# A 128-byte shift of the weight ring: padding behind the inverse-transform table of an attention and spectral-mixing kernel

## The chip, the cores and the metric

The kernel runs on one core of one Trainium2 chip. A core has a matrix engine (PE, or TensorE), a vector engine (DVE), a scalar engine (ACT), a general engine (POOL, or GpSimd) and a synchronising engine (SP); they run side by side and meet at semaphores. Sixteen DMA engines carry data between the chip's main memory and the core's working memory, which has 128 partitions. An address below is a byte offset within a partition; a tile of so many bytes per partition occupies the same offsets in all of them. Matrix products are summed in a second, small memory, PSUM.

The metric is the device time of one execution in microseconds (us), lower is better. A comparison counts as faster or slower from a difference of 2% on.

## The reference

Causal attention with a bias that decays with a running sum, followed by a spectral mixing layer: a Fourier transform over the sequence, one complex matrix per frequency for 64 frequencies, the inverse transform, a residual, and a channel product with a ReLU. Cut to what matters:

```python
def _attn_ref(q, k, v, s):                      # q, k, v: (8, 8, 576, 64)
    scores = scale * np.matmul(q, k.transpose(0, 1, 3, 2))
    cum = np.cumsum(np.maximum(s, 0.0), axis=-1)
    bias = -(cum[:, :, :, None] - cum[:, :, None, :])
    scores = np.where(causal, -1e9, scores + np.minimum(bias, 0.0))
    # ... softmax over the keys ...
    return np.matmul(attn, v)

def _moe_ref(x, w_r, w_i, w_ch):                # x: (8, 576, 512); w_r, w_i: (64, 512, 512)
    X = np.fft.rfft(x, axis=1)
    Xr, Xi = np.real(X[:, :64]), np.imag(X[:, :64])
    Yr = np.einsum('bmd,mde->bme', Xr, w_r) - np.einsum('bmd,mde->bme', Xi, w_i)
    Yi = np.einsum('bmd,mde->bme', Xr, w_i) + np.einsum('bmd,mde->bme', Xi, w_r)
    y = np.fft.irfft(Y, n=S, axis=1)            # Y is zero beyond 64 frequencies
    u = x + y
    return u + np.maximum(u @ w_ch, 0.0)
```

The two weight arrays hold 64 x 512 x 512 float32 numbers each, 67 MB, and each number is used once for each of the eight batches. They are by far the most of what has to be read.

## The kernel before

All tiles that live through the whole kernel come from one pool, in this order, and the weight ring comes right behind them:

```python
    gp = ctx.enter_context(tc.tile_pool(name="globals", bufs=1))
    x_all = gp.tile([P, NG, B, NT, P], FP16, name="x_all")
    y_acc = gp.tile([P, NCK, DM], FP32, name="y_acc")
    xs = [gp.tile([P, 2, 2, 2, 2, B, HM], BF16, name=f"xs{i}") for i in range(2)]
    # ...
    ident16h = gp.tile([P, P], FP16, name="ident16h")
    Ff_sb = gp.tile([P, NT, 3 * NM], FP16, name="Ff_sb")
    G_sb = gp.tile([P, S], FP16, name="G_sb")
    wch_sb = gp.tile([P, DT, DM], FP16, name="wch_sb")
    wpool = ctx.enter_context(tc.tile_pool(name="w_sb", bufs=WA))      # WA = 11
    wpool2 = ctx.enter_context(tc.tile_pool(name="w2_sb", bufs=WB))    # WB = 6
```

Here P = 128, S = 576, DM = 512, NT = 5 and SP = NT * P = 640. `G_sb` is the table of the inverse transform: 128 rows (64 frequencies, real and imaginary) of 576 half-precision numbers, which is 1152 bytes per partition. Places are given out one behind the other, so the length of `G_sb` sets where all later tiles begin.

A weight tile has 4096 bytes per partition. The weights are read as float32 and written as bfloat16 by transfers that POOL issues, two for each tile, each filling 64 partitions with two rows of 2048 bytes. The first eight tiles lie in parts of `y_acc` and `x_all` that aren't needed yet; all later ones lie in the ring:

```python
    def loads_w(upto):
            # ...
            i = ring_of(len(wt))
            if i is None:
                t = early[len(wt)]
            else:
                t = (wpool, wpool2)[i].tile([P, WM, DM], BF16, name="w_sb", tag="w")
            # ...
            for h in range(2):
                first = 1 if ri == 1 and m0 + h == 0 else 0
                todo.append((
                    t[HP * h : HP * h + HP, 2 * first :].rearrange("p (m q) e -> p m (q e)", q=2),
                    src[m0 + h + 2 * first : m0 + MC // 2 : 2, g * P : (g + 1) * P, :].rearrange(
                        "m (p q) e -> p m (q e)", q=2
                    ),
                ))
    # ...
        for _, (dst, src) in sorted(todo, key=lambda t: t[0]):
            nc.gpsimd.dma_start(out=dst, in_=src)            # L234: weights, q, k and v
```

The attention's own tiles come behind the ring: q, k and v, also loaded at L234, and the tile `v4` for the last 64 tokens of v:

```python
    v2 = [ap_.tile([P, 2 * NWN * W + P], FP16, name=f"v2_{i}") for i in range(NV)]
    v4 = [ap_.tile([P, B, VW], FP16, name=f"v4_{i}") for i in range(2)]      # VW = 66
    # ...
    t = loaded[n] = loaded[n + 1] = qkpool.tile([P, 2, R * D], BF16, name="qk2", tag="qk2")
```

The products with the weights (L463) start as soon as a tile has landed. After the last weight tile comes the end of the kernel: the inverse transform reads `G_sb` as stationary operand, and the results are summed in slots of the same ring and stored:

```python
    def add_y(dst, i, which, rows=slice(0, P), start=False, xx=(0, 1)):
            # ...
                nc.tensor.matmul(                                             # L744
                    dst[x][r, :], G_sb[rows, bass.ds(T * P, r.stop - r.start)],
                    yv[rows, bb, which, :], start=start, stop=True, skip_group_check=True,
                    tile_position=(0, r.start),
                )
    # ...
    def result(i):
        if i == 0:
            t = finpool.tile([P, 4 * DM], BF16, name="r_sb", tag="r", bufs=3)
        else:
            t = wpool.tile([P, WM, DM], BF16, name="r_w", tag="w").rearrange("p m e -> p (m e)")
        return t.bitcast(FP32).rearrange("p (x e) -> p x e", x=2)
    # ...
            dst = out[b, bass.ds(first_token(b, T + (x or 0)), P * (2 if x is None else 1)), :]
            nc.sync.dma_start(out=dst.rearrange("(x p) e -> p x e", p=P), in_=o)    # L828
```

Of the kernel before, what the change touches and what calls it, by code (L numbers as in the profile page):

```python
# [10 lines left out]
FP16 = mybir.dt.float16  # L11
# [7 lines left out]
def kernel(  # L19
# [11 lines left out]
    nc = tc.nc  # L31
    B, H, S, D = q.shape
    NM = moe_w_r.shape[0]
    DM = H * D
    P = 128
# [6 lines left out]
    SP = NT * P  # L42
# [45 lines left out]
    d_G = nc.inline_tensor(G_np, name="c_Ginv").ap()  # L88
# [8 lines left out]
    gp = ctx.enter_context(tc.tile_pool(name="globals", bufs=1))  # L97
# [6 lines left out]
    xs_flat = [t.rearrange("p q k h r b m -> p (q k h r b m)") for t in xs]  # L104
    ident16h = gp.tile([P, P], FP16, name="ident16h")
    Ff_sb = gp.tile([P, NT, 3 * NM], FP16, name="Ff_sb")
    G_sb = gp.tile([P, S], FP16, name="G_sb")
    wch_sb = gp.tile([P, DT, DM], FP16, name="wch_sb")
    wpool = ctx.enter_context(tc.tile_pool(name="w_sb", bufs=WA))
    wpool2 = ctx.enter_context(tc.tile_pool(name="w2_sb", bufs=WB))  # L110
# [154 lines left out]
    load(loads_w(W0), loads_v(0) + loads_tails(0) + first[2:] + loads_v(1))  # L265
    nc.sync.dma_start(out=Ff_sb, in_=d_Ff.rearrange("(T p) c -> p T c", p=P))
    nc.sync.dma_start(out=ident16h, in_=d_ident16h)
    nc.sync.dma_start(out=G_sb, in_=d_G)

    zero = ap_.tile([P, 16], FP32, name="zero")  # L270
    nc.vector.memset(zero, 0.0)
# [15 lines left out]
    with tc.tile_pool(name="cum_psum", bufs=1, space=PSUM) as cpsum:  # L287
# [5 lines left out]
            out=cum, data0=spos, data1=zer, initial=0.0, op0=ALU.add, op1=ALU.add  # L293
# [16 lines left out]
        for x in range(2):  # L310
            rows = slice(NL * x, NL * x + NL)
            nc.vector.tensor_copy(
                out=cumt4[rows, :], in_=cumt_sb[rows, NK, x::2]
# [653 lines left out]
```

## Time and profile before

| What | Value |
|---|---|
| time, median of 3 runs | 445.85 us (445.59 to 446.06) |
| span of the profiled execution | 443.9 us |
| PE busy | 339.8 us (77%) |
| DVE busy | 253.0 us (57%) |
| POOL busy | 246.2 us (55%) |
| ACT busy | 226.1 us (51%) |
| weight transfer of 256 KB from issue to landing, real and imaginary part | 8.4 and 8.9 us |
| store of 512 KB from issue to landing | 3.3 us |

The busy time of an engine is the time in which it works on an instruction; an engine that is idle in between waits for another one or for a transfer. The table alone doesn't tell which of them sets the time. For that, one has to see what the DMA engines do over the span, and which waits stand in the chain of work that ended last. GB/s in the profile count the bytes as written; where a transfer turns float32 into a 16-bit type, it reads twice as many. KB of a transfer are counted in the same way.

### The profile page before, as it was taken

The numbers are of one execution on the slowest core, as the hardware profiler recorded it, in microseconds if no ns is written. First come the engines' busy times: TensorE is split into PE (matmuls) and PEld (weight loads), VectorE is DVE, ScalarE is ACT, GpSimd is POOL, SyncE is SP. The second block draws the span as 40 slices with busy tenths as digits, with TensorE's granted clock in tenths as the row PEclk, the third lists the DMA queues.
The fourth block names the chain that finished last, engine by engine and source line by source line (L and its number), as shares of the span: only waits on it lengthen the run. The fifth ranks groups of instructions, "written<-read, shape, count | busy, mean of one in ns | idle before, by whom it ended". The sixth has DMA issues, their size and how long they took to land.

```text
span 443.9 us, 10783 instructions
## 1 busy us (share of the span) xinstructions
PE 339.8 (77%) x4364; PEld 206.9 (47%) x4411; DVE 253.0 (57%) x574; ACT 226.1 (51%) x421; POOL 246.2 (55%) x385
## 2 busy tenths in 40 slices
PE   1787888988686996593947828888887896859993
PEld 0465655656354553362625515565553455423441
DVE  7677775667545664462633605767655455432795
ACT  1477885467544743472633505765650444321793
POOL 7766666555565656365656546465544444530594
PEclk9999998999969898888895968999997999988998
DMA  9999999999999999999999999999999999996598
GB/s 181 202 207 205 204 207 205 206 206 205 209 192 205 205 209 204 209 206 208 204 207 206 209 206 202 206 206 203 205 209 210 210 209 210 209 217 122 179 373 324
DMA packets 72768, 93.25 MB, mean 210 GB/s; under 512 B 29760, under 2 KB 31296, under 8 KB 72720
## 3 DMA queue, kind: packets, MB, share of 16 engines
q0 software_dynamic: 63408, 81.29, 104.5%
q1 hardware_dynamic: 9312, 11.29, 7.8%
q8 instruction: 34, 0.56, 0.5%
q14 instruction: 14, 0.11, 0.1%
HBM read 163.51 MB, written 9.44 MB: 390 GB/s over the span
## 4 chain that ended last, share of the span: by engine, by line
DMA 67%; PE 16%; POOL 6%; DVE 5%; issue 4%; ACT 1%; POOLq 0%; DVEq 0%
DMA w_sb<-in_moe_w_i_dram 36%; DMA w_sb<-in_moe_w_r_dram 16%; DMA qk<-in_k_dram 10%; PE yp L463 3%; DMA x_all<-in_moe_w_r_dram 2%; POOL w_sb L234 2%; PE sc_ps L382 2%; DMA y_acc<-in_moe_w_r_dram 2%; PE sc_ps L376 2%; PE tr_ps L340 1%; POOL v L234 1%; PE u_ps L774 1%; PE av_ps L418 1%; PE z_ps L744 1%; DVE qt L344 1%
## 5 line engine op out<-in xcount | busy, mean ns | idle before, releaser
L390 ACT ACTIVATE p_sb<-sc_ps,cumt_sb 128x576 f16<-128x576 f32 (+1 forms) x256 | 141.5, 635 | 33.2 <-PE sc_ps L382 32.8
L234 POOL DMA_DIRECT2D w_sb<-in_moe_w_r_dram x120 | 71.2, 595 | 60.3 <-DMA w_sb<-in_moe_w_i_dram 16.1
L234 POOL DMA_DIRECT2D w_sb<-in_moe_w_i_dram x120 | 71.0, 593 | 53.2 <-DMA w_sb<-in_moe_w_i_dram 21.9
L344 DVE COPY qt<-tr_ps 64x576 bf16<-64x576 bf16 x64 | 47.8, 747 | 58.6 <-PE tr_ps L340 58.6
L234 POOL DMA_DIRECT2D v<-in_v_dram x72 | 52.0, 722 | 40.2 <-DMA w_sb<-in_moe_w_r_dram 9.6
L382 PE MATMUL sc_ps<-qt,kt 128*128 128x320 bf16 (+2 forms) x337 | 66.5, 302 | 6.7 <-ACT kt L344 2.7
L340 PE MATMUL tr_ps<-ident,qk 64*64 64x64 bf16 x1152 | 35.3, 206 | 40.9 <-DMA qk<-in_k_dram 17.6
L463 PE MATMUL yp<-w_sb,xs 128*32 128x512 bf16 (+1 forms) x480 | 43.2, 412 | 23.4 <-DMA w_sb<-in_moe_w_i_dram 16.6
L361 ACT ACTIVATE p<-sc_ps,cumt 128x64 f16<-128x64 f32 x32 | 10.0, 313 | 90.0 <-PE sc_ps L357 90.0
L376 PE MATMUL sc_ps<-negm,ident 128*128 128x256 bf16 x256 | 54.2, 297 | 0.0
L382 PEld LDWEIGHTS <-kt 128*128 128x128 bf16 x384 | 38.8, 106 | 31.3 <-ACT kt L344 8.9
L340 PEld LDWEIGHTS <-qk 64*64 64x64 bf16 x1152 | 26.9, 119 | 56.9 <-DMA qk<-in_k_dram 18.5
L418 PE MATMUL av_ps<-v,p_sb 128*128 128x65 f16 x1024 | 43.4, 196 | 1.4 <-DVE x_all L428 0.7
L418 PEld LDWEIGHTS <-p_sb 128*128 128x128 f16 x1024 | 36.8, 99 | 8.5 <-DVE x_all L428 3.9
L463 PEld LDWEIGHTS <-xs 128*32 128x32 bf16 (+1 forms) x512 | 19.2, 144 | 41.1 <-DMA w_sb<-in_moe_w_i_dram 15.3
L453 DVE CAST xs<-ft_ps 64x128 bf16<-64x128 f32 x128 | 36.6, 286 | 3.1 <-PE ft_ps L443 1.7
L423 DVE TENSOR_REDUCE den<-av_ps 128x5 f32<-128x10 f32 x64 | 10.8, 169 | 39.9 <-PE av_ps L418 38.9
L428 DVE TENSOR_TENSOR x_all<-av_ps,rcp 128x320 f16<-128x320 f32 x64 | 31.5, 492 | 2.2
L344 ACT COPY kt<-tr_ps 64x576 bf16<-64x576 bf16 x32 | 22.8, 714 | 15.2 <-DVE qt L344 14.6
L648 PE MATMUL z_ps<-wch_sb,xs 128*128 128x512 f16 x96 | 25.6, 415 | 0.2 <-DVE xs L639 0.2
L443 PE MATMUL ft_ps<-Ff_sb,x_all 128*64 128x192 f16 (+1 forms) x320 | 24.3, 266 | 1.0 <-DVE x_all L428 1.0
L344 DVE COPY kt<-tr_ps 64x576 bf16<-64x576 bf16 x32 | 24.4, 762 | 0.4
(113 smaller groups left out, 423.2 us busy)
## 6 DMA issues: line engine op xcount, KB each, us to landing
w_sb<-in_moe_w_r_dram POOLq DMA_DIRECT2D x120, 256.0 KB, 8.4
w_sb<-in_moe_w_i_dram POOLq DMA_DIRECT2D x117, 256.0 KB, 8.9
out_dram<-r_w SPq DMA_DIRECT2D x16, 512.0 KB, 3.3
v<-in_v_dram POOLq DMA_DIRECT2D x72, 64.0 KB, 7.4
qk<-in_q_dram POOLq DMA_DIRECT2D x15, 288.0 KB, 8.3
qk<-in_k_dram POOLq DMA_DIRECT2D x15, 288.0 KB, 9.2
x_all<-in_moe_w_i_dram POOLq DMA_DIRECT2D x6, 256.0 KB, 7.9
y_acc<-in_moe_w_r_dram POOLq DMA_DIRECT2D x4, 256.0 KB, 7.1
```

What stands on the lines that cost most here:

```text
L234: nc.gpsimd.dma_start(out=dst, in_=src)
L340: nc.tensor.transpose(ps[rows, r, :], src[rows, r, :], ident16[rows, rows])
L344: copy(out=to[:, :, :, half * RH : half * RH + RH], in_=ps[HP * i : HP * i + HP].rearrange("d r (h p) -> d h p r", h=2),)
L376: nc.tensor.matmul(ps[:, bass.ds(w * S, W)], ident16, negm[:, bass.ts(r, W)], start=True, stop=False, skip_group_check=True,)
L382: nc.tensor.matmul(ps[:, c0 : c0 + i1 - i0], keys[:, w, r, :], qh[:, i0:i1], start=False, stop=True, skip_group_check=True,)
L390: nc.scalar.activation(out=pt[:, poff[x] : poff[x] + S - w * W], in_=ps[:, w * S : (w + 1) * S - w * W], func=ACTF.Exp, bias=cumt_sb[:, x, ...
L418: nc.tensor.matmul(ps[:, I, r : r + NCH], lhsT, rhs, start=(i == 0), stop=(i == len(todo) - 1), skip_group_check=True,)
L428: nc.vector.tensor_tensor(out=x_all[:, g, b, :, D * h : D * h + D], in0=ps[:, :, 1 : NCH], in1=rcp.unsqueeze(2).to_broadcast([P, NT, D]), ...
L443: nc.tensor.matmul(ps[HP * q_ : HP * q_ + HP].rearrange("p h f -> p (h f)"), x_all[:nT, g, b, T, q_::2], Ff_sb[:nT, T, :], start=(T == 0), ...
L453: nc.vector.tensor_copy(out=xs[g % 2][HP * h : HP * h + HP, q_, :, h, :, b, :], in_=a)
L463: nc.tensor.matmul(ps[32 * cg : 32 * cg + 32, :], cols[k0:, q_, 1 - ri, :, c * MC // 2 + cg], wt[(g, c, ri, cg // 2)][k0:, 2 * (cg % 2) + ...
L648: nc.tensor.matmul(zs[i, x], xts[i][:, x, dt, :], wch_sb[:, dt, :], start=(dt == 0), stop=(last and dt == DT - 1), skip_group_check=True,)
```

## The change

The table gets SP = 640 columns in place of S = 576. The new ones, 128 bytes per partition, are neither loaded nor read. What comes behind the table then begins 128 bytes later. The purpose is that the slots of the weight ring and the tiles of the results begin at multiples of 512 bytes, which they miss by 128 bytes before.

```diff
@@ -104,7 +104,7 @@
     xs_flat = [t.rearrange("p q k h r b m -> p (q k h r b m)") for t in xs]
     ident16h = gp.tile([P, P], FP16, name="ident16h")
     Ff_sb = gp.tile([P, NT, 3 * NM], FP16, name="Ff_sb")
-    G_sb = gp.tile([P, S], FP16, name="G_sb")
+    G_sb = gp.tile([P, SP], FP16, name="G_sb")
     wch_sb = gp.tile([P, DT, DM], FP16, name="wch_sb")
     wpool = ctx.enter_context(tc.tile_pool(name="w_sb", bufs=WA))
     wpool2 = ctx.enter_context(tc.tile_pool(name="w2_sb", bufs=WB))
@@ -265,7 +265,7 @@
     load(loads_w(W0), loads_v(0) + loads_tails(0) + first[2:] + loads_v(1))
     nc.sync.dma_start(out=Ff_sb, in_=d_Ff.rearrange("(T p) c -> p T c", p=P))
     nc.sync.dma_start(out=ident16h, in_=d_ident16h)
-    nc.sync.dma_start(out=G_sb, in_=d_G)
+    nc.sync.dma_start(out=G_sb[:, :S], in_=d_G)
 
     zero = ap_.tile([P, 16], FP32, name="zero")
     nc.vector.memset(zero, 0.0)
```

## The prediction

> **What bounds the kernel now.** I read the page's slices and queues first, then the chain of waits, then busy time by stretches, then the chain inside one late stretch, and last the single packets of the trace.
>
> ```profile
> DMA  9999999999999999999999999999999999996598
> DMA packets 72768, 93.25 MB, mean 210 GB/s; under 512 B 29760, under 2 KB 31296, under 8 KB 72720
> ...
> q0 software_dynamic: 63408, 81.29, 104.5%
> q1 hardware_dynamic: 9312, 11.29, 7.8%
> ...
> HBM read 163.51 MB, written 9.44 MB: 390 GB/s over the span
> ...
> DMA 67%; PE 16%; POOL 6%; DVE 5%; issue 4%; ACT 1%; POOLq 0%; DVEq 0%
> ```
>
> To see: the 16 DMA engines are full in 36 of 40 slices. Nearly all of it is queue q0, the loads that GpSimd issues; they read float32 and write bfloat16 or float16, so 163.51 MB read become some 81 MB written. The chain that ended last is 67% DMA.
>
> ```profile
> 35.00:107.00 72.00, 63.40 (x1036) 42.31 (x1049) 48.94 (x125) 47.22 (x90) 42.57 (x68) 0.98 1.20 206
> ...
> 300.00:398.00 98.00, 78.15 (x826) 45.83 (x829) 51.52 (x103) 41.43 (x75) 47.30 (x80) 0.95 1.13 209
> ...
> 425.00:444.00 19.00, 12.03 (x57) 4.51 (x55) 12.72 (x12) 11.74 (x23) 13.25 (x11) 0.90 0.93 345
> ```
>
> The columns are the stretch, its length, busy time of PE, weight load, DVE, ACT and POOL, granted clock, DMA share, and GB/s written. A share over 1 means that packets of one DMA engine overlap. No compute engine fills the first two stretches; DMA overfills them.
>
> ```profile
> 345.50 9.74 DMA w_sb<-in_moe_w_i_dram
> 355.24 0.28 issue
> 355.52 9.73 DMA w_sb<-in_moe_w_i_dram
> 365.25 0.28 issue
> 365.53 9.72 DMA w_sb<-in_moe_w_i_dram
> 375.25 0.28 issue
> 375.53 9.73 DMA w_sb<-in_moe_w_i_dram
> 385.27 0.28 issue
> 385.55 11.85 DMA w_sb<-in_moe_w_i_dram
> 397.41 0.04 issue
> 397.45 1.07 PE yp L463 x6
> ```
>
> This is the chain from 340 to 400 us: one weight transfer after another, 10.0 us apart, the last landing at 397.41. So the kernel is a load stream of 397.4 us, then a tail of 443.9 - 397.4 = 46.5 us of products, sums and stores.
>
> **What the single packets cost.** The trace also records each DMA packet. The commonest duration by size written, with twice the bytes read in q0:
>
> ```
> q0  2048 B x32512 173 ns (weights)   q0 256 B x16384 41 ns (v)
> q0  2304 B x4096  192 ns (q, k)      q0 128 B x4096  32 ns (v, last rows)
> q0  1024 B x512    98 ns (wch)       q1 2048 B x4624 84 ns (all but 16 are stores)
> q1  2304 B x192    93 ns             q1 384 B x640   22 ns (Ff table)
> ```
>
> The q0 rows lie on one line: (173 - 98) / (4096 - 2048) = 0.0366 ns per byte read, plus 23 ns. It gives 41.7 for v and 191.7 for q and k. That is 1 / 0.0366 = 27.3 GB/s per engine, 437 GB/s on 16. In q1 the line from 384 to 2304 bytes has 0.0370 ns per byte and puts a 2048-byte packet at 83.5 ns; the stores show 84.
>
> [...]
>
> **The change part by part.**
> (1) Program. Instruction order and number are the same on all five engines; G is still loaded as 128 rows of 1152 bytes and read with the same offsets. Removed and added work: 0 us. There should be 72768 packets again.
> (2) Addresses, from the memory maps of the two built programs. Tiles ahead of G (x_all, y_acc, xs, ident16h, Ff) and G itself stay. Everything behind it moves up by 128 bytes. Modulo 512, wch and all 17 slots of the two weight rings go from 384 to 0, and so do result tiles, yv and Gx, v rows from 128 or 384 to 256 or 0, q and k likewise. Modulo 256, all of these go from 128 to 0. The eight early weight tiles, in y_acc and x_all, stay at 128: the in-run control.
> (3) Cost of a misaligned weight write, if it is paid. A 2048-byte row at 128 modulo 256 touches nine blocks of 256 bytes, the first and last half used. [...] at the q1 slope that is an estimated 128 x 0.037 = 4.7 ns. Each DMA engine has (32512 + 16384 + 4096) / 16 = 3312 packets of weights, v, q and k, less some 124 in the early tiles, so at most 3188 x 4.7 = 15.0 us, all on the stream that sets the end.
> (4) Whether it is paid. Writing 2048 bytes at the 0.037 slope is 76 ns; the same packet's read of 4096 bytes is 150 ns. If the two sides run side by side, 4.7 ns on the shorter are hidden. The rows of v4, the last tokens of v, test this within the run: they are 132 bytes apart, starting at 128 or 160 modulo 256, so 3 of 8 rows in one buffer and 4 of 8 in the other cross a 256-byte boundary, about 44% of 4096 packets. Their durations are 32 ns in 3960 cases and 31 in the other 136. A cost of crossing would split them nearly in half. The Ff table says the same for q1: its 384-byte rows begin at 128 and at 0 modulo 256 by turns, three to two, and 571 of 640 packets take 22 ns. So I put 0 ns on step 3.
> (5) Gaps between packets. Eight transfers take 10.01 us, or 10010 / 64 = 156 ns per packet on each engine, against 150 of pure reading. All that any alignment could win here is 6 ns in 156, or 4%. But each transfer also has a 4-byte completion packet of 22 ns per engine, and 22 / 8 = 2.75 ns per data packet is already half of it. I put 0 on this too, with less certainty: packet times don't show the gaps.
> (6) Stores. There are 18, of 9.44 MB in all: 4608 packets of 84 ns, 288 per engine. If their misaligned reads cost 4.7 ns, that is 288 x 4.7 = 1.4 us; but they lie beside the tail's computation, and only the last 256 KB, 8 packets per engine, lies behind its last sum: 0.04 us. The backlog of the last few stores could make this 0.3 us. The line says 0.
> Sum: 0 us, stream 397.4 and tail 46.5 as before.
>
> **The rivals.**
> *A, alignment pays on the write side.* Steps 3 and 6 together: 15.0 + 0.3, so about 430.5 us. For it: the stream sets the end, so every nanosecond of a packet counts, and nearly all its destinations become aligned. Against: step 4. The straight line doesn't speak against it, since a cost that every misaligned packet pays alike would sit in its 23 ns. I give 5% to anything over 2%, and some 12% to a smaller part, by the gaps of step 5, of 1 to 6 us.
> *B, only the stores gain.* About 445.5 us. For it: 345 GB/s written in the last stretch, with DMA share 0.93, so its queue is nearly full. Against: 84 ns on the q1 line.
> *C, slower.* Tiles move as one block, with pitches of 4096 bytes kept, so no two ring slots change their relation; only their relation to x_all, y_acc and xs does. [...] Perhaps 446 to 448 us, 5%, and over 2% hardly at all.
> *D, a gain in loads that finds another bound.* PE is busy for 78.15 of 98 us in the last stretch of loads, so it has 20 us to spare there, and more in share than the 4% that A could take. This rival wouldn't hide A.
>
> **Range and chances.** The sum says 445.85. I shade it by 0.25 for A and B, which are likelier than C: 445.6 us. The three runs before spread 0.47 us. The range down to 443.5 takes in B and the small form of A; up to 446.8 takes in C's lower half and the spread. Over 2% faster means below 436.9, A nearly in full: 5%. Over 2% slower means above 454.8, for which I have no mechanism: 1%.
>
> **What would show each step right or wrong.** Step 1: packets and instructions equal. Step 4: weight packets at 173 ns, in the rings (aligned) as in the early tiles (not), and v at 41. Step 5: the last weight transfers still 10.0 us apart, the last landing at 397 and about 209 GB/s from 300 to 398. If that row goes to 217 with packets still at 173 ns, gaps were the cost, and I was wrong in step 5; if weight packets fall to 168, in step 4. Step 6: stores at 84 ns, a tail of 46.5 us. I'm wrong as a whole if the landing of the last weight moves by more than 3 us.

## The result: 444.1 us, 0.3% faster, and the profile after

| | before | after |
|---|---|---|
| time, median of 6 runs each | 445.54 us | 444.11 us |
| lowest to highest | 445.14 to 446.06 | 443.77 to 445.00 |
| ratio after / before, 95% interval | | 0.9969 (0.9956 to 0.9982) |
| span of the profiled execution | 443.9 us | 442.4 us |

The gain of 1.4 us is small, far inside the 2%, but clear of the noise. The page of the changed kernel, in the lines that were shown of the kernel before (slices, packets, queues, memory traffic, chain):

```profile
DMA  9999999999999999999999999999999999997498
DMA packets 72768, 93.25 MB, mean 211 GB/s; under 512 B 29760, under 2 KB 31296, under 8 KB 72720
...
q0 software_dynamic: 63408, 81.29, 104.9%
q1 hardware_dynamic: 9312, 11.29, 7.6%
...
HBM read 163.51 MB, written 9.44 MB: 391 GB/s over the span
...
DMA 60%; PE 19%; DVE 7%; POOL 6%; issue 4%; ACT 2%; POOLq 0%; DVEq 0%
```

Packets and bytes are the same. The share of q0, the loads, doesn't fall (104.5% before). The share of q1, which holds the stores, falls from 7.8% to 7.6% of a slightly shorter span. That is the first hint. The chain has less DMA in it (67% before), but that isn't time saved: it takes another road through the same stretches, in which the loads run at the same rate. The busy time by stretches shows this. Its columns are the stretch, its length, PE, weight load, DVE, ACT, POOL, clock, DMA share and GB/s:

```profile
35.00:107.00 72.00, 62.96 (x1012) 42.33 (x1023) 48.85 (x124) 46.80 (x88) 42.56 (x68) 0.96 1.20 206
300.00:398.00 98.00, 78.53 (x828) 45.82 (x832) 51.52 (x103) 41.44 (x75) 47.56 (x80) 0.95 1.13 209
425.00:440.00 15.00, 11.57 (x55) 4.32 (x53) 12.25 (x12) 11.27 (x23) 12.77 (x11) 0.99 1.03 400
425.00:444.00 19.00, 11.57 (x55) 4.32 (x53) 12.25 (x12) 11.27 (x23) 12.77 (x11) 0.89 0.86 332
```

The two stretches of loads run at 206 and 209 GB/s, exactly as before. The last row is lower than the 345 before only because more of the same bytes are stored before 425 us. Cut at 440 us, while they are all still under way, the same stretch of the kernel before reads:

```profile
425.00:440.00 15.00, 12.03 (x57) 4.51 (x55) 12.72 (x12) 11.74 (x23) 13.25 (x11) 1.00 1.02 378
```

The DMA share is 1.02 before and 1.03 after: the engines are full, and move 378 GB/s before and 400 after. The chain of the changed kernel, from 340 to 400 us and at its end:

```profile
375.99 9.74 DMA w_sb<-in_moe_w_i_dram
385.73 0.28 issue
386.01 10.89 DMA w_sb<-in_moe_w_i_dram
396.91 0.04 issue
396.95 1.07 PE yp L463 x4
...
438.07 0.02 issue
438.09 0.69 DVE r_w L821
```

The last transfer of this chain lands at 396.91, 0.5 us ahead of its like in the execution before (397.41). It isn't the last weight, which the prediction took it to be. In the packet records of the kernel before, 749 of the 32512 weight packets start after 397.41 us, and the last ends at 407.42; in the changed kernel the last ends at 407.13. Both chains leave these out because they run on over products, from 397.45 us on in the kernel before and from 396.95 in the changed one. In a kernel that comes below, with results at 256 modulo 512, the chain goes through the last of them:

```profile
397.54 10.01 DMA w_sb<-in_moe_w_i_dram
407.54 0.04 issue
```

So the load stream of the kernel before ends at 407.4 us, and its tail is 36.5 us long, not 46.5.

The last sum of the changed kernel ends at 438.09 + 0.69 = 438.78. In the kernel before the chain ends so:

```profile
438.53 0.02 issue
438.56 0.69 DVE r_w L821
```

That is 439.25. Behind the last sum nothing is computed, only stored: 443.9 - 439.25 = 4.65 us before, 442.4 - 438.78 = 3.62 us after. So 1.03 us of the gain lies behind the last sum, and 0.47 us ahead of it, of which 0.29 us is there at the last weight already. The list of transfers says the same of the stores. Its last column is the median time to landing; first before, then after:

```profile
out_dram<-r_w SPq DMA_DIRECT2D x16, 512.0 KB, 3.3
...
out_dram<-r_w SPq DMA_DIRECT2D x2, 256.0 KB, 3.7
```

```profile
out_dram<-r_w SPq DMA_DIRECT2D x16, 512.0 KB, 2.8
...
out_dram<-r_w SPq DMA_DIRECT2D x2, 256.0 KB, 2.7
```

The last two stores, of 256 KB, take 3.7 us before and 2.7 after: the 1.0 us again. The single packets settle where the time is spent:

```
packets          before                                  after
q0 2048 B        173 ns x26622, 172 x5602                173 ns x26528, 172 x5708
q0  256 B         41 ns x15067, 40 x1270                  41 ns x15047, 40 x1268
q1 2048 B         84 ns x2223 of 4624, rest mostly 85     84 ns x4459 of 4624
(stores)          to 93; mean 87.7                        mean 84.0
```

Load packets don't move. Of the stores' packets only half took 84 ns before; now nearly all do.

Theory S: a store whose rows begin off a multiple of 256 bytes is read more slowly from the working memory, and because the stores of the tail fill the DMA engines (share 1.02), the delay piles up behind the last sum. Theory L, the rival: the loads gain too, by gaps between packets or by the earlier landing seen above.

### The profile page after: what moved, and what is told of

It is laid out like the page before. It is cut to its first block, busy times and chain, and to the rows that moved or that the text cites. A ratio compares the mean times of both kernels' runs of the same rounds, so it can differ in the third digit from the quotient of the medians.

```text
span 442.4 us, 10783 instructions
## 1 busy us (share of the span) xinstructions
PE 340.4 (77%) x4364; PEld 208.2 (47%) x4411; DVE 253.3 (57%) x574; ACT 226.2 (51%) x421; POOL 246.1 (56%) x385
## 2 busy tenths in 40 slices
DMA packets 72768, 93.25 MB, mean 211 GB/s; under 512 B 29760, under 2 KB 31296, under 8 KB 72720
## 4 chain that ended last, share of the span: by engine, by line
DMA 60%; PE 19%; DVE 7%; POOL 6%; issue 4%; ACT 2%; POOLq 0%; DVEq 0%
DMA w_sb<-in_moe_w_i_dram 31%; DMA w_sb<-in_moe_w_r_dram 16%; DMA qk<-in_k_dram 8%; PE yp L463 4%; PE sc_ps L382 3%; DMA x_all<-in_moe_w_r_dram 2%; POOL w_sb L234 2%; DMA qk<-in_q_dram 2%; PE sc_ps L376 2%; DMA y_acc<-in_moe_w_r_dram 2%; PE z_ps L546 2%; DVE xt L538 2%; DVE xs L453 1%; PE z_ps L648 1%; PE av_ps L418 1%
## 5 line engine op out<-in xcount | busy, mean ns | idle before, releaser
L443 PE MATMUL ft_ps<-Ff_sb,x_all 128*64 128x192 f16 (+1 forms) x320 | 25.2, 274 | 1.0 <-DVE x_all L428 1.0
```

Source lines behind the costliest of these rows:

```text
L443: nc.tensor.matmul(ps[HP * q_ : HP * q_ + HP].rearrange("p h f -> p (h f)"), x_all[:nT, g, b, T, q_::2], Ff_sb[:nT, T, :], start=(T == 0), ...
```

## The experiments

**Which tiles matter.** Two kernels shift only one part. In the first, the first weight ring with its result tiles begins at 0 modulo 512, and everything behind that ring is back at 384:

```diff
-    G_sb = gp.tile([P, S], FP16, name="G_sb")
+    G_sb = gp.tile([P, S + 64], FP16, name="G_sb")          # 128 bytes
     # ...
     wpool = ctx.enter_context(tc.tile_pool(name="w_sb", bufs=WA))
+    padpool = ctx.enter_context(tc.tile_pool(name="pad_sb", bufs=1))
+    pad = padpool.tile([P, 192], FP16, name="pad")           # 384 bytes
+    nc.vector.memset(pad, 0.0)
     wpool2 = ctx.enter_context(tc.tile_pool(name="w2_sb", bufs=WB))
```

> First weight ring and its result tiles at 0 modulo 512, everything behind that ring back at 384 (loads of the second ring, q, k, v and two of the 18 result stores misaligned as before). Theory S (the stores read their rows in blocks of 256 bytes; only 1.0 us of the gain, behind the last sum, is real and it is all from the stores): time 444.1 to 444.6, store packets of r_w at 84 ns, 1.0 us between the kernel before and this one from the last sum to the end. Theory L (the loads' destinations matter): only 11 of 17 ring slots gain, q, k and v nothing, so at most half of the gain, 444.8 to 445.3.

Measured: 444.26 us, ratio to the kernel before 0.9975 (0.9963 to 0.9988). Store packets take 84 ns in 4305 of 4624 cases.

The second is the reverse: `G_sb` as before, and a pad of 128 bytes between the two rings.

> The reverse: first ring and its result tiles at 384 modulo 512 as before, everything behind it aligned (second weight ring, q, k, v, two of the 18 stores). Theory S: 445.2 to 445.7 like the kernel before, stores again at 85 to 93 ns in half of the cases, 4.6 us from the last sum to the end. Theory L: about half of the gain or more, 444.6 to 444.9, the last weight landing 0.3 us or more ahead of 397.4.

Measured: 445.35 us, ratio 0.9993 (0.9983 to 1.0002), 84 ns in 2403 cases. The stretch from 425 to 440 us, of the first and then of the second:

```profile
425.00:440.00 15.00, 11.98 (x57) 4.49 (x55) 12.66 (x12) 11.70 (x23) 13.19 (x11) 1.00 1.03 400
```

```profile
425.00:440.00 15.00, 11.87 (x57) 4.42 (x54) 12.54 (x12) 11.58 (x23) 13.07 (x11) 1.00 1.02 379
```

400 GB/s go with the first ring, in which the results lie. Aligning q, k, v and the second ring leaves the time where it was. Theory L's halves, 444.8 to 445.3 and 444.6 to 444.9, don't appear. The second kernel does show what misled me in the profile after: the last transfer of its chain lands at 396.84, 0.57 us ahead of the kernel before, as L expected, and its last weight packet ends at 406.90, 0.52 us ahead; its time is still not clearly lower. In the first, the two are at 397.43 and 407.42, as in the kernel before, and it is faster.

**256 or 512 bytes, and does it matter how far off?** Only the padding of `G_sb` is changed: 384 bytes bring ring and results to 256 modulo 512; 96 bytes to 480, or 224 modulo 256; 160 bytes to 32. Two assumptions, neither shown so far, are set against each other for rows off the boundary. In the block theory each further block of 256 bytes that a row touches costs alike. In the beat theory the bytes between the boundary and the row cost as if they were stored, so at 224 the rate would be 2048 / (2048 + 224) = 64/71 of the aligned one.

```diff
-    G_sb = gp.tile([P, S], FP16, name="G_sb")
+    G_sb = gp.tile([P, S + 192], FP16, name="G_sb")          # or S + 48, or S + 80
```

> Padding of 384 bytes, so that ring and result tiles begin at 256 modulo 512. Theory S with blocks of 256 bytes: as the changed kernel, 443.9 to 444.5, stores at 84 ns. Rival with blocks of 512 bytes, as the change words it: as the kernel before, 445.2 to 445.7.

> Padding of 96 bytes, so that ring and result tiles begin at 480 modulo 512, which is 224 modulo 256. Theory S with the rule that a row off the boundary fetches everything from the boundary on[...], so stores at 64/71 of the aligned 407 GB/s, 367, and about 7/4 of the 1.0 us loss: 445.6 to 446.4. Rival in which only crossing one more block counts, however little of it is used: as the kernel before, 445.2 to 445.7.

> Padding of 160 bytes: ring and result tiles begin at 32 modulo 256. Block theory: like the kernel before, 445.2 to 446.0, 376 to 382 GB/s in the stretch from 425 to 440 us. Beat theory: [...]444.2 to 444.8, about 394 to 400 GB/s.

Measured: at 256, 444.34 us, ratio 0.9975 (0.9964 to 0.9986). At 480, 446.01 us, 1.0014 (1.0003 to 1.0025). At 32, 446.02 us, 1.0015 (1.0007 to 1.0023). The same stretch, in this order:

```profile
425.00:440.00 15.00, 11.23 (x54) 4.13 (x51) 12.06 (x11) 10.93 (x22) 12.41 (x11) 0.95 1.03 400
```

```profile
425.00:440.00 15.00, 11.61 (x55) 4.33 (x53) 12.28 (x12) 11.31 (x23) 12.79 (x11) 1.00 1.03 379
```

```profile
425.00:440.00 15.00, 12.65 (x60) 4.80 (x58) 13.29 (x12) 12.37 (x25) 13.84 (x12) 1.00 1.01 378
```

So 256 bytes are enough, and the 512 of the change's wording isn't needed. Off the boundary, 32, 128 and 224 bytes give one and the same rate. A 2048-byte row touches eight blocks of 256 bytes when it begins on one and nine otherwise, and that count goes with the rate, 400 GB/s with eight and 378 to 379 with nine, while the distance from the boundary doesn't. Since every row off the boundary touches just one block more, these runs can't tell a cost per extra block from a fixed cost per row off the boundary. The beat theory, on which the 4.7 ns of step 3 of the prediction rest too, missed at both ends: it expected 367 GB/s at 480 and about 394 to 400 at 32, and measured are 379 and 378. The time at 480 lies in the range that it had given, but the rate doesn't, so the time isn't a point for it. Both kernels are some 0.15% slower than the kernel before at the same store rate. From the last sum to the end they take 4.59 and 4.63 us, as it does, so the excess isn't found there. In the profiled execution at 32 the last sum ends 0.62 us later than in the kernel before; that at 480 was a quick one, with a span of 443.4 us, and doesn't show the excess. Its cause stays open.

**The rates by themselves.** A kernel of transfers alone, which leaves out the whole computation and ran once: 16 stores of 512 KB at each offset, then 24 loads of float32 into float32, then 48 loads of half the size into bfloat16.

```diff
+    for off, to in zip((0, 32, 128, 224), [out] + twins):
+        o = src[:, off // 4 : off // 4 + 1024].rearrange("p (x e) -> p x e", x=2)
+        for i in range(16):
+            b, h = divmod(i, 2)
+            nc.sync.dma_start(out=to[b, 256*h : 256*h+256, :].rearrange("(x p) e -> p x e", p=P), in_=o)
+    # ... loads of moe_w_r on SP into f32[...][:, off // 4 : off // 4 + 1024], no change of type
+    # ... then loads of moe_w_i on POOL into b16[...] at the same byte offsets, float32 to bfloat16
```

> A kernel of transfers alone, which computes nothing of the reference: stores of 512 KB back to back from rows that begin 0, 32, 128 and 224 bytes past a multiple of 256, then float32 loads without a change of type into rows at the same four offsets, then loads that turn float32 into bfloat16, again at the four. Block theory (each further 256-byte block that a stored row touches costs the same, however little of it is used): 400 to 410 GB/s at 0, and 375 to 385 at 32, 128 and 224 alike. Beat theory (bytes fetched for nothing count): 400 at 32, 380 at 128, 365 at 224. For the float32 loads, where as much is written as read: if writing suffers like reading, 3% less off the boundary (17 blocks in place of 16); if only reads of the working memory suffer, the same at all four. For the type-changing loads both say the same at all four, 205 to 217 GB/s written.

Busy time by stretches, of which the last two columns count, DMA share and GB/s. Stores from 0, 32, 128 and 224 bytes past a multiple of 256:

```profile
6.00:20.00 14.00, 0.00 (x0) 0.00 (x0) 1.00 1.05 408
40.00:56.00 16.00, 0.00 (x0) 0.00 (x0) 1.00 1.02 378
62.00:76.00 14.00, 0.00 (x0) 0.00 (x0) 1.00 1.03 382
84.00:98.00 14.00, 0.00 (x0) 0.00 (x0) 1.00 1.03 378
```

Loads of float32 without a change of type, into rows at the same four offsets:

```profile
106.00:128.00 22.00, 0.00 (x0) 0.00 (x0) 1.00 1.03 413
136.00:158.00 22.00, 0.00 (x0) 0.00 (x0) 1.00 1.03 413
166.00:190.00 24.00, 0.00 (x0) 0.00 (x0) 1.00 1.03 410
196.00:220.00 24.00, 0.00 (x0) 0.95 (x5) 1.00 1.03 410
```

Stores lose 7% at 32 and at 224, 6% at 128. On each of 16 engines a 2048-byte packet takes a slot of 2048 x 16 / 408 = 80.3 ns on the boundary, 86.7, 85.8 and 86.7 off it: a row off the boundary costs 5.5 to 6.4 ns more, a little over half of an eighth of the aligned slot, 80.3 / 8 = 10.0 ns. The stores from 0 go to the output and the others to scratch tensors; the doubled stores below go to both in turn and show 408 and 379 GB/s as well, so the destination isn't the cause. Loads lose at most 0.7%, although here as much is written as is read. The loads that change type give 209 GB/s at all four offsets, with packets of 173 ns. So it is the reading side of the working memory that suffers, by 6 to 7%. On the writing side hardly anything shows, at most 0.7%; whether a misaligned write is free, or hidden beside the read of the same packet, isn't shown.

**Is it the rate, or a fixed cost of the last store?** Two pairs change how much is stored. The first pair stores every result twice, the second time to a scratch tensor:

```diff
     # ... the stores of the last tokens are doubled in the same way
-            dst = out[b, bass.ds(first_token(b, T + (x or 0)), P * (2 if x is None else 1)), :]
-            nc.sync.dma_start(out=dst.rearrange("(x p) e -> p x e", p=P), in_=o)
+            for to in (out, twin):
+                dst = to[b, bass.ds(first_token(b, T + (x or 0)), P * (2 if x is None else 1)), :]
+                nc.sync.dma_start(out=dst.rearrange("(x p) e -> p x e", p=P), in_=o)
```

> The kernel before, but every result is stored twice, the second time to a scratch tensor that nobody reads: 18.9 MB of stores in the tail, which they then bound. Rate theory: 18.9 MB at 379 GB/s is 49.8 us from the first store at 414 us on, so 463 to 470 us.

> The same doubling on the changed kernel. Rate theory: 18.9 MB at 400 GB/s in place of 379, so 2.2 to 3.2 us less than the doubled kernel before, twice the gain or more of the stores stored once. Rival, a fixed cost of the last store (its latency, not its rate): again about 1.0 to 1.5 us less, as without doubling.

Measured: 468.43 us (ratio to the kernel before 1.0525, 1.0507 to 1.0542) and 465.35 us (1.0454, 1.0436 to 1.0472), which is 3.1 us apart, at the upper end of the rate theory and two to three times what a fixed cost gives. The rate theory had put 400 GB/s; with the 408 that these stores reach, the 16.4 MB that start after 420 us give 16.4 MB x (1/379 - 1/408), an estimated 3.1 us. From 440 to 460 us, with the stores alone, misaligned and then aligned:

```profile
440.00:460.00 20.00, 0.00 (x0) 0.00 (x0) 0.00 (x0) 0.00 (x0) 0.00 (x0) 0.50 1.03 379
```

```profile
440.00:460.00 20.00, 0.00 (x0) 0.00 (x0) 0.00 (x0) 0.00 (x0) 0.00 (x0) 0.53 1.05 408
```

The second pair leaves out half of most stores; all sums are still computed:

```diff
             dst = out[b, bass.ds(first_token(b, T + (x or 0)), P * (2 if x is None else 1)), :]
+            if x is None and 2 <= i < last:
+                dst, o = dst[:P, :], o[:, 0:1, :]
             nc.sync.dma_start(out=dst.rearrange("(x p) e -> p x e", p=P), in_=o)
```

> The kernel before, but of the results of most pairs only the first 128 of 256 rows are stored (the other half is left out; all sums are computed; the first two pairs, the pair of last tokens and the last pair are stored whole). The stores then come slower than they are served at either alignment. Backlog theory: nothing queues ahead of the last stores, so the misalignment costs at most 0.2 us: 443.2 to 444.3. Rival, a fixed cost per store or of the last one: no faster than 444.9.

> The same halving on the changed kernel. Backlog theory: within 0.3 us of the halved kernel before, 443.0 to 444.2, and hardly faster than the changed kernel with full stores. Rival: 1.0 us or more faster than the halved kernel before.

Measured: 444.36 us (0.9968, 0.9959 to 0.9976) and 443.97 us (0.9968, 0.9956 to 0.9980). The medians are 0.39 us apart, a little over the 0.3 expected and the 444.36 a little over its range; the ratios don't tell them apart. The misaligned kernel is as fast as the aligned one once its stores no longer queue (DMA share 0.59 from 425 to 440 us, in place of 1.02), although its store packets still take 86.3 ns on average.

From the last sum (its start in the chain plus 0.69 us) to the end of the span, in all nine executions that store the results at most once:

| kernel | result tiles modulo 256 | us behind the last sum |
|---|---|---|
| before | 128 | 4.65 |
| all but the first ring aligned | 128 | 4.62 |
| at 480 | 224 | 4.59 |
| at 32 | 32 | 4.63 |
| after | 0 | 3.62 |
| first ring alone | 0 | 3.59 |
| at 256 | 0 | 3.57 |
| before, half of the stores | 128 | 3.15 |
| after, half of the stores | 0 | 3.15 |

So 1.0 us goes with the alignment of the results alone, and vanishes without a queue. The line of stores issued one after another shows why, in the kernel before; its columns are start and length:

```profile
419.08 16.27 SPq L828 DMA_DIRECT2D out_dram<-r_w  x13
```

The issue of one store takes 0.37 us, so 13 of them begin (16.27 - 0.37) / 12 = 1.32 us apart. A store of 524,288 bytes is served in 1.39 us at 378 GB/s and in 1.29 us at 408. The tail produces just between the two rates: misaligned stores fall behind by 0.07 us each, aligned ones keep up. That is also why the changed kernel shows 400 GB/s and not 408: it stores about as fast as the tail produces, 524,288 bytes in 1.32 us, or 397 GB/s. The packet records show the queue directly. Counted in order, the last packet of the store issued at 419.08 us ends 2.4 us after the issue, and that of the store issued at 437.60 us 3.4 us after it; in the changed kernel the same two take 2.3 and 2.4 us.

## Why the prediction was right, and which term was too small

The time, 444.11 us, lies in the range of 443.5 to 446.8, and the change is within 2%, to which the prediction left 94%. The direction wasn't forecast by the sum, which said 0. That the range reached down far enough is in part luck: rival B as sized reached 445.5, and the room below it was left for rival A, which is refuted. By the steps:

- Steps 1 and 2 held: 72768 packets again, the same instructions.
- Step 4, loads don't pay for misaligned rows, held: weight packets at 173 ns and v at 41 before and after, in the rings as in the early tiles. Rival A, some 15 us, is refuted: aligning loads gained nothing that could be measured, and the rates by themselves show 209 GB/s at each offset. My reason was only half right. I argued that the shorter write is hidden beside the longer read, which no run shows. Float32 loads, where both are equally long, lose at most 0.7% too.
- Step 5, no gain in the gaps, held: still 10.0 us between the weight transfers of the chain and 209 GB/s from 300 to 398. Its end of the load stream, 397.4 us, was misread from the chain; the sum of 0 doesn't depend on it. The last weight packet ends at 407.13, 407.25 and 407.27 us in the three executions of the table with all rings aligned, and at 407.42, 407.55, 407.62 and 407.64 in the four with none; but at 407.42 with the first ring alone, at 406.90 with all but the first, and with doubled stores at 407.18 (none) and 407.15 (all). A gain of some 0.3 us from aligned loads is neither shown nor excluded.
- Step 6 is the term that was mis-sized. I gave the stores 0, with 0.3 us as the most that a backlog could add, and measured is 1.0 us. Two things failed in it. First, I read 84 ns off as the commonest duration; half of the packets were longer, and the mean of 87.7 would have shown it. The cost itself came out nearly right: the 4.7 ns of step 3 stand beside a measured 5.5 to 6.4. But that a misaligned row costs 128 bytes more, from which they come, was not shown by any run, and the rates at 32 and 224 speak against it. Second, I let only the last 256 KB lie behind the last sum. In the trace of the kernel before, 585 store packets, 1.20 MB, end after it (0.84 MB in the changed kernel). With DMA engines full from 425 to 440 us (share 1.02), the delay of every store waits ahead of the last one. The stores are also 20, not 18: 16 of 512 KB and 4 of 256 KB. Bytes and packets were right.
- Rival B was the right mechanism at a third of its size: 445.5 us predicted, 444.1 measured. Of the 1.4 us, 1.0 is shown to be the stores'. The other 0.4 can't be told from the spread of the runs.
- Rival C, slower, didn't come with this change; its 446 to 448 us were a guess of mine, with no trace behind it. Rival D was not put to the test, since no large gain of the loads was there to be hidden.

Aligned results, at 0 or 256 modulo 512, are the best found. The three kernels that have them and store everything once lie at 444.1 to 444.3 us and can't be told apart.

## What to carry to other kernels

A buffer that transfers read should begin its rows at multiples of 256 bytes: rows of 2048 bytes were read here at 408 GB/s on the boundary and at 378 to 382 off it. Where transfers only write, alignment made no clear difference, at most 0.7%. It was worth time only where the stores fill the DMA engines at the end: compare the time between issues with the size of a store over its rate, 1.32 us against 1.39 and 1.29 here. And look at the mean and spread of packet durations, not at the commonest one: a cost that falls on half of the packets doesn't move the mode (84 ns before and after, in 2223 and 4459 of 4624).

## What the runs showed of the hardware that wasn't expected

- Reading rows of 2048 bytes from the working memory off a 256-byte boundary costs 6 to 7% of the rate (378 to 382 against 408 GB/s), and 32, 128 or 224 bytes off cost nearly alike. If the bytes between the boundary and the row set the cost, 224 would be seven times as dear as 32 (an estimate, 224 / 32). Measured is 6.4 ns more for a 2048-byte packet at both, so they don't set it.
- Writing to the working memory at the same offsets costs at most 0.7% (413, 413, 410 and 410 GB/s), so the two directions differ in what alignment costs.
- A slowed store doesn't show in every packet record. In the transfers alone, 50, 53 and 26% of the store packets at 32, 128 and 224 still take the aligned 84 ns, while the rate is lower by 6 to 7% over all.
